# An mLSTM with a feed-forward network on one core: first chunks' decays by TensorE, zeros' products between the groups, a new order of steps

## The chip, the cores and the metric

The kernel runs on one core of one Trainium2 chip. The metric is the device time of one execution in microseconds (us). Five queues work side by side and wait for each other through semaphores: TensorE (PE; its weight loads are PEld), VectorE (DVE), ScalarE (ACT), GpSimd (POOL), and SyncE (SP), which here issues all loads and stores.

## The reference

An mLSTM (4 batches, 8 heads, 768 steps, heads of 40) and behind it a feed-forward network of 320 to 2048 to 320 over all 3072 tokens. Inputs are scaled so that gates reach far into the negative: the exponents must keep full precision.

```python
for t in range(S):
    m_new = np.maximum(f_gate[:, :, t] + m, i_gate[:, :, t])
    f_stab = np.exp(f_gate[:, :, t] + m - m_new)
    i_stab = np.exp(i_gate[:, :, t] - m_new)
    m = m_new
    C = f_stab[..., None, None] * C + i_stab[..., None, None] * np.einsum('bhd,bhe->bhde', vt, kt)
    n = f_stab[..., None] * n + i_stab[..., None] * kt
    h_tilde = np.einsum('bhde,bhe->bhd', C, qt)
    denom = np.maximum(np.abs(np.einsum('bhd,bhd->bh', n, qt)[:, :, None]), 1.0)
    y[:, :, t] = sigmoid(o_gate[:, :, t]) * h_tilde / denom
...
h = x @ w_in                                   # x: y as 3072 tokens of 320
g = np.where(h >= 1, h, np.where(h <= -1, 0.0, (h + 1) ** 2 / 4))
return g @ w_out
```

## The kernel before, in words

**Chunks.** The recurrence is done in chunks of L = 128 steps: 6 chunks of time (c) for each of 4 batches (b), numbered n = 4c + b, 24 in all. Inside a chunk it is a masked attention. `gate_sums(c)` (step g) makes, for all 32 sequences of heads at once, the running maximum m, the clamped log-decays a, and their running sum `ac` (with a rest `al`); `gate_tail` (k) forms four exponents per step in `ex`; `gate_exps` (h) transposes them on TensorE and takes their exponential into G, and the negated sum into nA. The decay between steps s and t is exp(ac[t] − ac[s]) for t ≥ s. For this `ac` is stored to DRAM (`a_d`), and `load_A(n)` (A) loads it back, broadcast over the 128 partitions, as [128, 8 heads, 128]; `select` (e, POOL) puts −30000 where t < s; `decay` (x00, x01: two halves of four heads) adds nA as a bias and takes the exponential on ACT. `score_mm` (s) makes the products of k and q, `score_mul` (m) multiplies them by the decays on DVE, `scale1` (v) scales the values on POOL.

**The rest of a chunk** is the generator `main`: step u multiplies scores by values into `up` (16 narrow fp32 products), y divides by the normalizer and multiplies by the output gate (`sz`, then `y`), z transposes y on TensorE in three pieces, t copies it into `xh` (float32r) and `xl` (what float32r lost). The third piece is 128 columns of which 64 are a copy of columns made by a `tensor_copy` of y.

**The feed-forward part.** Four chunks make a group j of 512 tokens, six groups in all. For each j there are 16 slots fc: `mm1` multiplies by a 128-column piece of w_in into a PSUM bank `psh` (8 products of 512 columns), ACT and DVE apply the activation (r), `parts` splits it into `gh` and `gl`, `mm2` adds to four banks `pso`. The weights come as 64-bit words and are converted on the chip in 16 pieces (`convert`: `words` on ACT, DVE and POOL, then `split` with a cast on ACT and a subtraction on DVE), two of them ahead of the first slot and the others in j = 0. Chunks of the next group are worked on between the slots of the present one by `slot(i)`.

**Order.** The framework's scheduler orders each engine's instructions by a planner's times, except where `InOrder.on` makes every new instruction of an engine follow the one before it. That is so for the front: the list `STEPS` (line 53) is walked by a loop (line 645) that issues loads (L.), the steps above for n = 0 to 3, the gates of the first three chunks of time, two conversions (c), and `warm(k)` (w): k products of zeros (128 x 128 by 128 x 512, bfloat16), of no use for the result. After the list come `load_og(1)`, `load_A(4)` to `load_A(6)` and the first `slot` calls, which follow the last marked copies of step t. All these have line L78 or L81 of the helper in the profile.

**PSUM.** `psum_a` (line 300) hands out banks in the front by turns: two `psa`, one `psh` and four `pso` in a cycle of seven; the eighth bank holds the transposed gates.

Of the kernel before, what the change touches and what calls it, by code (L numbers as in the profile page):

```python
# [51 lines left out]

STEPS = (
# [41 lines left out]
def mlstm_ffn_kernel(ctx, tc, qk, qn, vk, og, fi, w_in, w_out, cst, out):  # L95
# [20 lines left out]


    cs_t = const.tile([P, P + 9 * D1 + 2], F32, name="cs")
    ident = cs_t[:, :P]
    bmask = cs_t[0:120, P:P + 9 * D1].rearrange("p (g x) -> p g x", g=3)  # L120
# [4 lines left out]
    a_d = dr.tile([NSEQ, S], F32, name="a_d")  # L125
# [19 lines left out]
    rst = const.tile([NSEQ, L], F32, name="rst")  # L145

    def load_gates(pool, c0, c1):
        n = (c1 - c0) * L
        sl = slice(c0 * L, c1 * L)
        t = pool.tile([NSEQ, 2, n], F32, name="fi_t", bufs=1 if c0 == 0 else 1)  # L150
        nc.sync.dma_start(t, fi[:, :, sl])
        fg_t, ig_t = t[:, 0, :], t[:, 1, :]
        if c0 == 0:
            nc.gpsimd.memset(rst, 1.0)
            nc.gpsimd.memset(rst[:, 0:1], 0.0)
        for c in range(c0, c1):
            gsrc[c] = pool, ig_t[:, (c - c0) * L:][:, :L], fg_t[:, (c - c0) * L:][:, :L]
# [10 lines left out]
    def gate_sums(c):  # L168
        pool, i, f = gsrc.pop(c)
        new = lambda name, p=NSEQ, n=L, bufs=1: pool.tile([p, n], F32, name=name, bufs=bufs)  # L170
        k = 1
        m, a, ah, ac, al = new("m", n=L + 1, bufs=k), new("a", bufs=k), new("ah", bufs=k), new("ac", bufs=3), new("al", bufs=k)

        ex = exs[c] = new("ex", P, bufs=2)
        nc.vector.tensor_copy(m[:, 0:1], carry)
        nc.vector.tensor_tensor_scan(out=m[:, 1:], data0=f, data1=i, initial=carry, op0=ALU.add, op1=ALU.max)
# [5 lines left out]
        nc.vector.tensor_tensor_scan(out=ac, data0=rst, data1=ah, initial=0.0, op0=ALU.mult, op1=ALU.add)  # L182
# [18 lines left out]
    def gate_exps(c):  # L201
        ex = exs.pop(c)
        if c < 3:
            if c == 0:
                T["gates"] = ps_h.tile([P, 512], F32, name="psh")
            tp = T["gates"][:, c * P:(c + 1) * P]
        else:
            tp = psum_a()[:, :P]
# [61 lines left out]
    def convert(kind, i):  # L270
        raw = raws.pop((kind, i))
        if kind == "in":
# [27 lines left out]
    def psum_a():  # L300
# [80 lines left out]
    def load_A(n):  # L381
# [4 lines left out]
        t["A"] = gate.tile([P, H, L], F32, name="A3") if n == 3 else ld.tile([P, H, L], F32, name="Abc", bufs=3)  # L386
        src = a_d[b * H:(b + 1) * H, c * L:(c + 1) * L]
# [23 lines left out]
    def decay(n, hh):  # L411
# [72 lines left out]
    def main(n):  # L484
# [16 lines left out]
        up = psum_a()  # L501
        if n < SPLIT_FROM:
# [29 lines left out]
        nc.vector.tensor_tensor(out=y[:, :DM].rearrange("p (h d) -> p h d", d=D), in0=hv[:, :, 0:D], in1=sz, op=ALU.mult)  # L532
        nc.vector.tensor_copy(y[:, DM:], y[:, 2 * P:DM])
# [18 lines left out]
        nc.vector.tensor_tensor(out=xh[64:128, 2, cs], in0=xv[64:128, 2, :], in1=xh[64:128, 2, cs].bitcast(F32),  # L552
# [239 lines left out]
```

## Time and profile before

| | |
|---|---|
| median of 3 runs (lowest to highest) | 535.79 us (535.57 to 537.06) |
| the profiled execution | 533.05 us, span of its instructions 531.3 us |
| mean granted clock of TensorE | 0.959 |
| busy: PE, PEld | 496.6 us (93%), 425.4 us (80%) |
| busy: DVE, ACT, POOL | 377.1 us (71%), 300.3 us (57%), 150.8 us (28%) |
| moved by DMA | 53.37 MB |

"Busy" is the time in which an engine has at least one instruction running; instructions of one engine overlap a little, so a sum of durations is some per cent above it. In a row of the timeline the first number is the start in us, the second the time covered, and x7 means seven instructions run together. In a row by stretches come, after the stretch and its length, the busy time and the count of instructions of PE, PEld, DVE, ACT and POOL, then the granted clock, the DMA engines' share and GB/s.

### The profile page before, as it was taken

What the parts mean: (1) busy time and instruction counts of PE and PEld (TensorE: products, weight loads), DVE (VectorE), ACT (ScalarE), POOL (GpSimd) and SP (SyncE); (2) the same over time, 40 slices, a digit from 0 to 9 for tenths busy, and PEclk for the clock granted to TensorE, in tenths of its full rate; (3) what the DMA queues carried; (4) which work ended last, traced back from release to release, by engine and by line L of the source; (5) the groups of instructions that cost most, each with busy time, mean ns of one, the idle gap of its engine ahead of it and who ended that gap; (6) DMA issues with size and microseconds to landing.
All of it is one profiled execution on the core that took longest, in us unless ns stands there. A gap on an engine that the chain in (4) does not pass through costs nothing.

```text
span 531.3 us, 9265 instructions
## 1 busy us (share of the span) xinstructions
PE 496.6 (93%) x3552; PEld 425.4 (80%) x3552; DVE 377.1 (71%) x710; ACT 300.3 (57%) x592; POOL 150.8 (28%) x139
## 2 busy tenths in 40 slices
PE   7976999888998999999999789799999999999996
PEld 3664778867887889879889668688997898989985
DVE  6479799999978677868577749586766676543332
ACT  5635885666586364568363444754459344455553
POOL 1435264251541225342135415034311212000000
PEclk9965899998999999999999989899999999999999
DMA  5997675472431213441213423032433100010001
GB/s 179 319 290 199 177 245 169 134 232 72 149 102 42 55 52 103 133 151 30 68 37 104 118 85 104 11 97 79 114 105 115 40 1 1 1 51 1 0 1 50
DMA packets 51449, 53.37 MB, mean 100 GB/s; under 512 B 10157, under 2 KB 44365, under 8 KB 51405
## 3 DMA queue, kind: packets, MB, share of 16 engines
q1 hardware_dynamic: 51405, 52.78, 32.8%
q8 instruction: 28, 0.46, 0.3%
q14 instruction: 16, 0.13, 0.1%
HBM read 48.72 MB, written 4.06 MB: 99 GB/s over the span
## 4 chain that ended last, share of the span: by engine, by line
PE 64%; DVE 19%; ACT 7%; DMA 4%; issue 3%; POOL 1%; SPq 0%; ACTq 0%; POOLq 0%; DVEq 0%
PE psh L78 28%; PE pso L78 25%; PE psa L78 11%; DVE gl L78 2%; ACT Abc L78 2%; DVE r L78 2%; DVE ow L78 2%; DMA A<-a_d 2%; DVE C L78 1%; ACT r L78 1%; DMA Abc<-a_d 1%; DVE mg L78 1%; DVE win L78 1%; DVE z L78 1%; DVE m L78 1%
## 5 line engine op out<-in xcount | busy, mean ns | idle before, releaser
L78 ACT ACTIVATE r<-psh,half 128x512 f32<-128x512 f32 x96 | 65.4, 685 | 95.0 <-PE psh L78 91.9
L78 PE MATMUL psh<-xh,wh 128*128 128x512 f32 x288 | 105.0, 418 | 9.6 <-DVE r L78 5.2
L78 PE MATMUL pso<-oh,gh 128*128 128x320 f32 x368 | 113.4, 316 | 0.4 <-ACT r L78 0.4
L78 PE MATMUL pso<-ow,gh 128*128 128x320 f32 x368 | 113.3, 312 | 0.0
L78 DVE SCALAR_TENSOR_TENSOR r<-psh,r 128x512 f32<-128x512 f32 x96 | 65.9, 686 | 59.6 <-ACT r L78 59.1
L78 PE MATMUL pso<-oh,gl 128*128 128x320 f32 x368 | 104.7, 311 | 0.0
L78 PE MATMUL psh<-xh,wl 128*128 128x512 f32 x288 | 102.4, 407 | 0.0
L78 DVE TENSOR_TENSOR gl<-r,gh 128x512 fp32r<-128x512 f32 x92 | 71.6, 780 | 31.8 <-ACT gh L78 30.9
L78 ACT CAST gh<-r 128x512 fp32r<-128x512 f32 x92 | 56.8, 618 | 63.5 <-DVE r L78 62.8
L78 PEld LDWEIGHTS pso<-oh,gh 128*128 128x128 f32 x368 | 68.7, 188 | 5.0 <-ACT r L78 0.6
L78 PEld LDWEIGHTS pso<-ow,gh 128*128 128x128 f32 x368 | 69.2, 188 | 3.5
L78 PEld LDWEIGHTS pso<-oh,gl 128*128 128x128 f32 x368 | 66.8, 188 | 0.5
L78 PEld LDWEIGHTS psh<-xh,wh 128*128 128x128 f32 x288 | 51.5, 194 | 18.8 <-DVE r L78 6.5
L78 PEld LDWEIGHTS psh<-xh,wl 128*128 128x128 f32 x288 | 55.7, 195 | 12.3 <-DVE wl L78 0.2
L78 ACT ACTIVATE Abc<-Abc,nA 128x128 f32<-128x128 f32 x160 | 49.3, 389 | 24.8 <-POOL Abc L78 19.4
L78 PE MATMUL psh<-xl,wh 128*128 128x512 f32 x192 | 62.0, 405 | 0.0
L78 ACT ACTIVATE r<-r 128x512 f32<-128x512 f32 x96 | 60.2, 632 | 2.3
L78 POOL TENSOR_TENSOR m<-m 128x1024 bf16<-128x1024 f32 x16 | 32.6, 2037 | 55.4 <-DVE m L78 49.3
L78 POOL TENSOR_TENSOR C<-C,dec 120x369 f32<-120x369 f32 x16 | 14.6, 916 | 106.5 <-PE psa L78 106.5
L78 POOL TENSOR_TENSOR v<-vk,G 128x328 f32<-128x328 f32 x36 | 31.3, 876 | 46.8 <-issue 30.8
L78 PEld LDWEIGHTS psh<-xl,wh 128*128 128x128 f32 x192 | 37.1, 194 | 8.6
L78 PE MATMUL psa<-raw 40*128 40x128 f32 x304 | 30.5, 294 | 0.9 <-DVE hv L78 0.9
(166 smaller groups left out, 723.2 us busy)
## 6 DMA issues: line engine op xcount, KB each, us to landing
Abc<-a_d SPq DMA_DIRECT2D x23, 512.0 KB
raw<-in_qk SPq DMA_DIRECT2D x48, 160.0 KB
vk<-in_vk SPq DMA_DIRECT2D x20, 324.0 KB
wraw<-in_w_in SPq DMA_DIRECT2D x8, 768.0 KB
wraw<-in_w_out SPq DMA_DIRECT2D x8, 640.0 KB
sig<-in_og SPq DMA_DIRECT2D x6, 640.0 KB
out<-r SPq DMA_DIRECT2D x24, 160.0 KB
qn<-in_qn SPq DMA_DIRECT2D x20, 180.0 KB
```

The lines of the kernel that those rows point to most:

```text
L78: r = getattr(self.engine, name)(*args, **kwargs)
```

## The change

1. **Decays of chunks 0 to 3.** The first gates are loaded on 96 partitions (`fi0`: the 32 sequences three times). The sums `ac` stand there three times; two subtractions of the upper 16 bits (`top`) leave in the three blocks the three bfloat16 parts of the sum. `exponents(b)` (A0 to A3) puts into PSUM the mask (identity times `late_t`, −30000 where t < s) and adds, per head, a product of `pick`, which chooses the head's three rows, with the three parts. `decay` then reads PSUM. `first_sums` (p) transposes the sums for nA, which DVE reads. No store, broadcast load or `select` is left for these chunks; the others keep them, from an `a_d` whose rows of one chunk of time lie together.
2. **Zeros' products.** Instead of `warm` at a place of its own, `heat` is set by w and `hot(out)` issues that many zeros' products at the beginning of the next group, into the bank that the group then overwrites. The list has w9, w3 and then ones and twos between nearly all groups.
3. **Order.** The list is new. The second and third chunks' gates (k1, h1, g2, k2, h2) and the second conversion stand behind t3; the conversion is parted into c (words) and d (split), both in order.
4. **y.** It has 320 columns; the third transposition takes its last 128, so the copy goes, and the last subtraction of t writes the other half of `xh`'s third block. For c = 0 POOL makes `sz`.
5. **Smaller.** First chunk's copies into `ex` on POOL instead of ACT, one more copy into `ex` there for all chunks; `ident` and the block mask are loaded separately; psum_a's cycle is eight banks, with two of `psh`.

```diff
 STEPS = (
-    "w8 w2 Lf Lc Lo Lq0 g0 k0 A0 Lq1 o A2 h0 A1 w8 Lv0 Lq2 Lw0 s0 w6 Lq3 w2 w3 Lv2 A3 s1 g1 e0 "
-    "v0 x00 k1 Lw1 x01 m01 m00 w2 e1 v1 x10 x11 m10 u0 s2 e2 v2 x21 e3 c m11 y0 x20 m20 w4 m21 v3 u1 "
-    "w7 s3 y1 x31 z0 x30 t0 u2 z1 m31 w2 m30 u3 w1 y2 t1 c y3 z2 t2 h1 z3 g2 k2 w1 t3 w4 h2 "
+    "Lg Lo Li Lq0 Lv0 Lq1 Lw0 Lf Lq2 Lv2 Lq3 Lw1 Lc o w9 g0 p w3 A0 k0 x00 w1 s0 m00 w1 A1 h0 x01 v0 m01 x10 w1 s1 "
+    "v1 m10 x11 m11 w2 u0 w2 A2 y0 c x20 w1 s2 x21 v2 m20 w1 u1 z0 m21 w2 t0 y1 g1 d w2 A3 x30 w1 s3 x31 v3 m30 w1 u2 "
+    "z1 m31 w2 t1 y2 w1 u3 z2 w2 t2 y3 z3 w2 t3 k1 h1 c d g2 k2 h2 "
 )
...
-    a_d = dr.tile([NSEQ, S], F32, name="a_d")
+    a_d = dr.tile([NC, NSEQ, L], F32, name="a_d")
...
+    def first_gates():
+        t = gate.tile([3 * NSEQ, 2, L], F32, name="fi0")
+        nc.sync.dma_start(t, fi0)
+        gsrc[0] = gate, t[:, 1, :], t[:, 0, :]
...
-        nc.sync.dma_start(a_d[:, c * L:(c + 1) * L], ac)
-        nc.scalar.copy(ex[64:96], ac)
+        if c > 0:
+            nc.sync.dma_start(a_d[c], ac)
+            nc.scalar.copy(ex[64:96], ac)
+        else:
+            for p in (2 * NSEQ, NSEQ):
+                nc.vector.tensor_tensor(out=ac[:p], in0=ac[:p], in1=top(ac[:p]), op=ALU.subtract)
+            T["ac"] = ac
+            m, a, ah, ac, al, i = (x[2 * NSEQ:] for x in (m, a, ah, ac, al, i))
+            nc.gpsimd.tensor_copy(ex[64:96], ac)
...
+    def top(x):
+        return x.bitcast(BF16).rearrange("p (t w) -> p t w", w=2)[:, :, 1]
+
+    def first_sums():
+        tp = psum_a()
+        hot(tp)
+        tp = tp[:, :NSEQ]
+        nc.tensor.transpose(tp, T["ac"][2 * NSEQ:], ident[2 * NSEQ:3 * NSEQ, 2 * NSEQ:3 * NSEQ])
+        nc.vector.tensor_scalar(out=nA[:, 0, :], in0=tp, scalar1=-1.0, scalar2=None, op0=ALU.mult)
+
+    def exponents(b):
...
+        ps = T[n]["Ap"] = [psum_a() for _ in range(2)]
+        hot(ps[0])
+        for hh in range(2):
+            nc.tensor.matmul(ps[hh], idb, late_t.unsqueeze(1).broadcast_to([P, 4, P]), start=True, stop=False)
+        for hh in range(2):
+            for h in range(4):
+                k = b * H + 4 * hh + h
+                nc.tensor.matmul(ps[hh][:, h * L:(h + 1) * L], pick[:, k:k + 1].broadcast_to([3 * NSEQ, P]),
+                                 top(T["ac"]), start=False, stop=h == 3)
...
-    def warm(k):
-        out = psum_a()
-        for _ in range(k):
+    heat = 0
+    def hot(out):
+        nonlocal heat
+        for _ in range(heat):
             nc.tensor.matmul(out, zeros[:, :P], zeros, start=True, stop=True)
+        heat = 0
...
-            nc.scalar.activation(A[:, h, :], A[:, h, :], AF.Exp, bias=bias)
+            src = T[n]["Ap"][hh][:, (h - 4 * hh) * L:][:, :L] if c == 0 else A[:, h, :]
+            nc.scalar.activation(A[:, h, :], src, AF.Exp, bias=bias)
...
-        nc.vector.tensor_tensor(out=sz, in0=sg.rearrange("p (h d) -> p h d", d=D),
+        mark["x", "pool"] = (nc.vector if c else nc.gpsimd).tensor_tensor(out=sz, in0=sg.rearrange("p (h d) -> p h d", d=D),
                                                      in1=z.unsqueeze(2).broadcast_to([P, H, D]), op=ALU.mult)
-        y = wk.tile([P, 3 * P], F32, name="y", bufs=2)
...
-        nc.vector.tensor_copy(y[:, DM:], y[:, 2 * P:DM])
...
-        for k in range(3):
+        hot(xp)
+        for k in range(2):
             nc.tensor.transpose(xp[:, k * P:(k + 1) * P], y[:, k * P:(k + 1) * P], ident)
+        nc.tensor.transpose(xp[:, 2 * P:3 * P], y[:, DM - P:], ident)
...
         elif what[0] == "c":
-            mark["c", "act"], mark["c", "dve"] = nc.scalar.last, nc.vector.last
-            InOrder.on = False
-            split_next("c")
-            InOrder.on = True
+            rest = convert(*W_ORDER[nw])
+            load_w(*W_ORDER[nw + 2])
+            nw += 1
+        elif what[0] == "d":
+            rest()
```

More of the change, by code (lines that the diff above doesn't have):

```diff
@@ L94, in mlstm_ffn_kernel @@
 @with_exitstack
-def mlstm_ffn_kernel(ctx, tc, qk, qn, vk, og, fi, w_in, w_out, cst, out):
+def mlstm_ffn_kernel(ctx, tc, qk, qn, vk, og, fi0, fi, w_in, w_out, cst, out):
     nc = Core(tc)
@@ L115, in mlstm_ffn_kernel @@
     nc.gpsimd.memset(zeros, 0.0)
-    cs_t = const.tile([P, P + 9 * D1 + 2], F32, name="cs")
-    ident = cs_t[:, :P]
-    bmask = cs_t[0:120, P:P + 9 * D1].rearrange("p (g x) -> p g x", g=3)
+    ident = const.tile([P, P], F32, name="ident")
+    cs_t = const.tile([120, 9 * D1], F32, name="cs")
+    bmask = cs_t.rearrange("p (g x) -> p g x", g=3)
+    idb = gate.tile([P, P], BF16, name="idb")
+    nc.gpsimd.affine_select(out=idb, in_=zeros[:, :P], pattern=[[1, P]], compare_op=ALU.not_equal, fill=1.0,
+                            base=0, channel_multiplier=-1)
+    pick = gate.tile([3 * NSEQ, NSEQ], BF16, name="pick")
+    for g in range(3):
+        nc.gpsimd.affine_select(out=pick, in_=pick if g else zeros[:3 * NSEQ, :NSEQ], pattern=[[1, NSEQ]],
+                                compare_op=ALU.not_equal, fill=1.0, base=g * NSEQ, channel_multiplier=-1)
+    late_t = gate.tile([P, P], BF16, name="late_t")
+    nc.gpsimd.affine_select(out=late_t, in_=zeros[:, :P], pattern=[[1, P]], compare_op=ALU.is_ge, fill=-30000.0,
+                            base=0, channel_multiplier=-1)
     half = const.tile([P, 1], F32, name="half")
     nc.vector.memset(half, 0.5)
-    a_d = dr.tile([NSEQ, S], F32, name="a_d")
+    a_d = dr.tile([NC, NSEQ, L], F32, name="a_d")
     G = const.tile([P, NC, P], F32, name="G")
@@ L202, in gate_exps @@
         ex = exs.pop(c)
[L203 to L208, printed above, removed]
+        tp = psum_a()[:, :P]
         nc.tensor.transpose(tp, ex, ident)
         nc.scalar.activation(G[:, c, :], tp, AF.Exp)
-        nc.scalar.mul(nA[:, c, :], tp[:, 64:96], -1.0)
         if c > 0:
+            nc.scalar.mul(nA[:, c, :], tp[:, 64:96], -1.0)
             decays(c, c + 1)
+    def top(x):
[7 more added lines that the diff above has]
+    def exponents(b):
+        n = b
+        T.setdefault(n, {})["A"] = (gate.tile([P, H, L], F32, name="A3") if n == 3 else
+                                    ld.tile([P, H, L], F32, name="Abc", bufs=3))
+        ps = T[n]["Ap"] = [psum_a() for _ in range(2)]
[7 more added lines that the diff above has]
+                                 top(T["ac"]), start=False, stop=h == 3)
     def decays(c0, c1):
@@ L275, in convert @@
             words(w, raw)
-            split(wh[:, :, sl], wl[:, :, sl], w)
+            return lambda: split(wh[:, :, sl], wl[:, :, sl], w)
         else:
@@ L280, in convert @@
             if 2 * i >= PLAIN_FC:
-                split_out(i)
+                return lambda: split_out(i)
+        return lambda: None
     def split_out(i):
@@ L385, in load_A @@
         t = T.setdefault(n, {})
-        t["A"] = gate.tile([P, H, L], F32, name="A3") if n == 3 else ld.tile([P, H, L], F32, name="Abc", bufs=3)
-        src = a_d[b * H:(b + 1) * H, c * L:(c + 1) * L]
+        t["A"] = ld.tile([P, H, L], F32, name="Abc", bufs=3)
+        src = a_d[c, b * H:(b + 1) * H]
         mark[n, "A"] = nc.sync.dma_start(t["A"], src.unsqueeze(0).broadcast_to([P, H, L]))
@@ L501, in main @@
         up = psum_a()
+        hot(up)
         if n < SPLIT_FROM:
@@ L647, in mlstm_ffn_kernel @@
         hh = int(what[2:] or 0)
-        if what == "Lf":
-            load_gates(gate, 0, 3)
+        if what == "Lg":
+            first_gates()
+        elif what == "Lf":
+            load_gates(gate, 1, 3)
         elif what == "Lc":
-            nc.sync.dma_start(cs_t, cst)
+            nc.sync.dma_start(cs_t, cst[0:120, P:])
+        elif what == "Li":
+            nc.sync.dma_start(ident, cst[:, :P])
         elif what == "Lo":
@@ L670, in mlstm_ffn_kernel @@
         elif what[0] == "A":
-            load_A(n)
+            exponents(n)
+        elif what[0] == "p":
+            first_sums()
         elif what[0] == "v":
@@ L675, in mlstm_ffn_kernel @@
             sigmoid(0)
-        elif what[0] == "e":
-            select(n)
         elif what[0] == "x":
@@ L699, in mlstm_ffn_kernel @@
     for i in range(FRONT - EARLY, FRONT):
-        with behind(("x", "act"), ("x", "dve")):
+        with behind(("x", "act"), ("x", "dve"), ("x", "pool")):
             slot(i)
```

66 lines of the change are left out of this document (39 added, 27 removed).

## The prediction

> **What bounds the kernel now.** I read the page's slices first, then busy times by stretch, then the chain that ended last in the opening stretch.
>
> ```profile
> span 531.3 us, 9265 instructions
> ...
> PEclk9965899998999999999999989899999999999999
> ```
> ```profile
> core 0: us, PE busy (x) PEld busy (x) DVE busy (x) ACT busy (x) POOL busy (x), PEclk, DMA share, GB/s
> 0.00:51.74 51.74, 41.32 (x218) 26.27 (x219) 35.65 (x98) 25.94 (x68) 20.93 (x26) 0.80 0.85 253
> 51.74:139.60 87.86, 82.06 (x477) 69.56 (x476) 83.27 (x136) 61.31 (x120) 33.82 (x31) 0.95 0.52 165
> 139.60:216.00 76.40, 74.33 (x573) 65.81 (x572) 58.03 (x109) 46.22 (x90) 24.94 (x21) 1.00 0.27 80
> ```
>
> The first row is the front, the part that the step list orders: it ends when the last copy of the fourth chunk (step t3) is made, at 51.74. The second row is the first 16 feed-forward slots (they end where ACT finishes its 16th reading of a product, 139.60); in it DVE is busy 83.27 of 87.86 us, idle only 4.59. That stage converts the weights on DVE, so it ends when DVE's list is done. In the third row DVE is at 58.03 of 76.40 and TensorE at 74.33: from there TensorE leads. So what the change is worth is read from one balance: DVE's work up to 139.60 is 35.65 + 83.27 = 118.92, its idle time 16.09 + 4.59 = 20.68. A front that ends earlier helps only as far as one of the two shrinks.
>
> ```profile
> 5.49 2.76 DMA a_d<-ac
> ...
> 10.07 7.49 DMA Abc<-a_d
> 17.57 10.11 DMA A<-a_d
> ...
> 28.87 2.44 ACT A L81 x8
> ```
>
> These are rows of the chain of waits: the sums go to DRAM (5.49) and return broadcast; the fourth chunk's copy lands only at 27.68, and eight exponentials take 2.44. The change removes these trips.
>
> **The change part by part: DVE's work.** Durations are of this execution (span 531.3, its own time 533.05, the median of the runs shown 535.79, so 2.74 above it).
>
> ```profile
> L81 DVE TENSOR_TENSOR sz<-sig,z 128x320 f32<-128x320 f32 x4 | 2.2, 560 | 0.1
> ...
> L81 DVE COPY y<-y 128x64 f32<-128x64 f32 x4 | 0.8, 194 | 0.1
> ```
> ```profile
> 10.49 0.28 DVE L81 TENSOR_TENSOR a<-fi_t,m 32x128 f32<-32x128 f32 x1
> ...
> 11.93 0.15 DVE L81 TENSOR_TENSOR dc<-ac,al 32x1 f32<-32x1 f32 x1
> ...
> 37.53 0.86 DVE L78 TENSOR_SCALAR win<-wraw 128x768 uint16<-128x768 uint16 x1
> 38.29 1.08 DVE L78 TENSOR_SCALAR mg<-mg 128x768 f32<-128x768 f32 x1
> ...
> 39.48 0.95 DVE L78 SCALAR_TENSOR_TENSOR win<-mg,win 128x768 int32<-128x768 int32 x1
> ...
> 41.62 1.27 DVE L78 TENSOR_TENSOR wl<-win,wh 128x768 fp32r<-128x768 f32 x1
> ...
> 43.45 3.34 POOL L78 TENSOR_SCALAR_AFFINE_SELECT Abc<-Abc 128x1024 f32<-128x1024 f32 x3
> ...
> 44.19 0.14 DVE L81 COPY m<-carry 32x1 f32<-32x1 f32 x1
> ...
> 45.86 1.06 DVE L81 TENSOR_TENSOR a<-a,m 32x128 f32<-32x128 f32 x1
> ...
> 50.82 0.15 DVE L81 TENSOR_TENSOR dc<-ac,al 32x1 f32<-32x1 f32 x1
> ...
> 51.44 0.29 DVE L81 TENSOR_TENSOR xh<-pso,xh 64x128 fp32r<-64x128 f32 x1
> ```
>
> Gone from DVE: four copies of y in the front (0.8) and four more before 139.60 (another 0.8), and four products sz that POOL takes (2.2). New: two subtractions that part the sums (0.28 each, like row 10.49, since only the partitions grow) and nA read on DVE (0.15 by row 11.93), less one small copy (0.14): +0.6. Net −3.2. Merely moved behind t3: the tail of the second chunk's gates (10.49 to 12.08, 1.6), the second weight conversion (0.86 + 1.08 + 0.95 + 1.27 = 4.2) and the third chunk's gates (44.19 to 50.97, 6.8). They free t3 but stay on DVE's list, so I credit them at nothing; what would be lost if they weren't covered is those 12.6 us, now due between t3 and the sixteenth slot. POOL's masking of the later chunks goes with them: row 45.86 shows a DVE step of 0.28 taking 1.06 while the three masks of row 43.45 run. Four masks vanish from POOL, but they ran mostly while DVE waited. I carry that slowing over unchanged, bounded by 3.3 us either way (the three masks' length).
>
> **DVE's idle time in the new front.** Every engine keeps the step list's order, so I walk the queues with these rows.
>
> ```profile
> 1.72 3.19 PE L81 MATMUL psa<-zeros 128*128 128x512 bf16 x7
> ...
> 11.44 2.08 PE L81 MATMUL pso<-raw 40*128 40x128 f32 x16
> ...
> 20.31 0.74 POOL L81 TENSOR_TENSOR ow<-ow,G 128x328 f32<-128x328 f32 x1
> ...
> 24.93 1.68 PE L81 MATMUL pso<-zeros 128*128 128x512 bf16 x7
> ...
> 26.54 1.16 PE L81 MATMUL pso<-raw 40*128 40x128 f32 x16
> ...
> 28.02 1.88 PE L81 MATMUL psa<-ow,Abc 128*128 128x41 f32 x16
> ...
> 35.30 3.63 PE L81 MATMUL pso<-ow,A 128*128 128x41 f32 x16
> ...
> 40.03 0.48 ACT L81 CAST xh<-pso 128x384 fp32r<-128x384 f32 x1 [5.05 <-PE pso L81]
> ```
> ```profile
> DVE m L81 <- DMA fi_t<-in_fi: 2.3, 1, 2.3
> ```
>
> The pairs show each product at half and at full clock: a zeros' product 0.43 or 0.24, a score group 2.08 or 1.16, a chunk's output group 3.63 or 1.88. No row has the new exponents' products. They are bfloat16 as the zeros are, two of 512 columns and eight of 128, so I estimate by columns (0.43 and a quarter of it): 1.7 at half clock, 1.0 at full. Both ends: 0.9 (weights hidden) and, if each of the ten cost as much as a zeros' product, 4.3; the zeros are the nearest row. The waits that follow:
>
> 1. Start: the sums wait for their gates as now, 0.8 + 2.3 = 3.1.
> 2. Chunk 0. The sums' parts are ready at about 6.1. TensorE then has a transposition (as one zeros' product, 0.43), three zeros (1.3) and the exponents (1.7): the first half at 9.1. ACT's four exponentials, half of 2.44, end at 10.3. DVE's gate work ends at 8.6; with the score group behind, it waits 2.6. ACT's next entry is the gates' exponential, and TensorE reaches its transposition only after scores 0 and the next exponents, at 12.5 to 14.5; so x01 waits too, and DVE 2.3 again, then twice 0.5 (1.22 on ACT against 0.69 on DVE). Together 5.9.
> 3. sz on POOL: y's last step waits for it, and DVE with all that is queued behind y (conversion, gates, score products). 0.74 to 0.9 and two handovers: 1.0 four times, 4.0.
> 4. On ACT the second chunk's two copies of sums (g1) and the weight cast (d) stand ahead of x30, so chunk 3's exponentials start near 30 although its exponents are in PSUM at 24: DVE waits 1.1 for the cast and 0.8 for the two halves.
> 5. Transposition, cast (0.48) and handovers ahead of t2 and t3: 1.2 each, 2.4.
> 6. While ACT is late, TensorE has nothing from about 28 to 33, and I expect half clock from there: +1.2.
>
> Sum 3.1 + 5.9 + 4.0 + 1.9 + 2.4 + 1.2 = 18.5, against 16.1 now. DVE's work up to t3 is 35.65 − 1.6 − 4.2 − 6.8 − 2.4 = 21, so t3 ends near 40 instead of 51.74. Loads don't set it: 253 GB/s moved in the first row, and the first four chunks' loads, with 2 MB of broadcasts gone, are 4.6 MB, in by some 20 us. SP's queue loses four issues that waited for the sums' store; fi0, ident and cs are three small ones more. The relaid a_d merges rows of 512 B; its later loads hide behind 0.52 of DMA share.
>
> After t3:
>
> ```profile
> DVE Abc L78 <- PE psa L78: 1.5, 1, 1.5
> ...
> 53.55 1.22 PE L78 MATMUL psh<-xh,wh 128*128 128x512 f32 x2 [0.21 <-DVE Abc L78]
> ```
>
> Now DVE idles 4.59 there, 1.5 of it for the next chunk's scores at a cold clock. With 12.6 us of backlog at hand I take 3.0 (ends 1.0 and 4.6).
>
> **The sum.** 118.9 − 3.2 + 18.5 + 3.0 = 137.2 for 139.6: 2.4 earlier. Behind it sixteen copies of y go, 16 × 0.194 = 3.1 of DVE time where TensorE leads; a quarter counts, 0.8. Together 3.2 us: 529.9 for the profiled 533.05, and 532.6 beside the median. About 0.3%, 1.6 us, is what a measurement of this kernel can tell from no change.
>
> **The clock.**
>
> ```profile
> 3.38:6.79 3.41, 2.39 (x6) 0.60 (x4) 3.09 (x12) 0.94 (x3) 0.00 (x0) 1.00 0.93 336
> ...
> 13.60:17.03 3.43, 3.43 (x9) 1.22 (x8) 1.24 (x2) 2.10 (x8) 0.00 (x0) 1.00 1.24 303
> ...
> 27.27:30.68 3.41, 2.93 (x29) 2.57 (x27) 2.30 (x7) 1.81 (x7) 2.03 (x2) 1.00 0.81 255
> 30.68:57.99 27.31, 20.37 (x77) 14.74 (x79) 23.26 (x52) 14.38 (x44) 10.75 (x10) 0.50 0.71 210
> ```
>
> The record shows a clock of 1.00 from the start, but the zeros' 0.43 says half; it rises after the stretch 13.60 to 17.03, which zeros and scores filled, and falls after 27.27 to 30.68, though TensorE was busy 2.93 of 3.41 with narrow products. Two to three zeros a group may not be enough to raise it or hold it. The Trainium skill, TensorE: Matmul & The Clock Gate, Part 1, says that one busy window of about 3.4 us lifts the gate and one idle window lowers it again. By that rule the clock would hold until the pause at 28, as step 6 has it; the trace disagrees on the fall, which came after a window 86% busy, and that speaks for the second rival below.
>
> **The rivals.**
> - *TensorE, not DVE, sets the first stage.* It is busy 82.06 of 87.86 there, which speaks for it; that its loads are busy 69.56 (79%) against 65.81 of 76.40 (86%) in the next stage speaks against. Then the first product's start counts: 53.55 becomes some 42 to 44, and allowing for a cold start the gain is 8 to 9: about 527. It needs DVE's backlog to fit in the gaps.
> - *The clock stays at half through the front (slower).* Place: between chunk 0's exponents and u3. The doubled groups are then 4 × (0.7 + 0.9 + 1.75) + 28 zeros × 0.19 + transpositions 4 × 0.3 = 20 us more on TensorE, which becomes the front's bound: t3 near 52, DVE idle near 29 instead of 18.5, so 10.4 later than the sum, 543; if it falls only from 20 us on, about 537 to 539. It decides once DVE's idle exceeds 23.5. For: the fall at 30.68. Against: more zeros in the gaps than in that window, which had none.
> - *Nothing to measure.* The removed trip is replaced by waits 2 to 4 in full and the clock rises as late as 17: idle 20 to 22, 534.5 to 537.
> - *The exponents' products don't shorten chunk 0* (each ten cost 4.3): 2.6 more in step 2 and again in part for chunk 1; this is inside the case before.
>
> **How the numbers follow.** Forecast 0.43 (own range 529.5 to 534); TensorE's case 0.15; nothing to measure 0.22; half clock 0.20. Faster 0.58, same 0.22, slower 0.20. The range 527 to 539 takes in the first three and the milder part of the last, and leaves out some 0.06 below and 0.12 above.
>
> **What would show it.** Right: no load of the sums for chunks 0 to 3, t3 near 40, the first wide product near 42, DVE idle 17 to 20 up to t3 with waits on POOL of 0.8 to 1.0 four times, the sixteenth slot read near 137. Wrong: zeros' products of 0.43 behind 20 us (the clock), t3 far from 40, or DVE idle by more than 5 us between t3 and the sixteenth slot, which would mean that TensorE sets the stage.

## The result, and the profile after

The changed kernel takes 552.45 us (median of 4 runs, 548.6 to 554.7) against 536.42 for the kernel before (4 runs, 535.57 to 537.53): a ratio of 1.029, with an interval of 1.0216 to 1.0364. It is slower by 16 us, where 3 us less were forecast, and lies 13 us above the range. The profiled execution took 550.32 us, its span is 548.5.

The page of the changed kernel, its span and the granted clock in 40 slices:

```profile
span 548.5 us, 9300 instructions
...
PEclk9956579998899999999999979999999999999999
```

The same kernel by stretches: the front up to the last copy t3, the first 16 feed-forward slots, and the rest. In between stands one stretch of the second row by itself.

```profile
core 0: us, PE busy (x) PEld busy (x) DVE busy (x) ACT busy (x) POOL busy (x), PEclk, DMA share, GB/s
0.00:42.95 42.95, 30.71 (x210) 21.27 (x210) 23.58 (x67) 16.62 (x44) 14.85 (x30) 0.82 0.75 224
42.95:155.50 112.55, 91.46 (x504) 76.11 (x505) 93.04 (x159) 68.52 (x139) 40.50 (x39) 0.84 0.44 141
52.53:66.04 13.51, 0.00 (x1) 0.03 (x1) 11.64 (x26) 6.79 (x16) 6.50 (x5) 0.58 0.60 202
155.50:548.52 393.02, 373.59 (x2861) 329.75 (x2859) 254.60 (x461) 212.86 (x406) 95.08 (x86) 0.98 0.22 66
```

t3 ends at 42.95 instead of 51.74, 8.8 us earlier. The 16th slot is read at 155.50 instead of 139.60, 15.9 later, and the rest takes 393.02 instead of 391.68. So the front gained, and the stage behind it lost 24.7. DVE's work up to the 16th slot is 23.58 + 93.04 = 116.62 (118.92 before). Its idle time is 42.95 − 23.58 = 19.37 up to t3 and 112.55 − 93.04 = 19.51 behind it, where before had 4.59. The third row shows the largest pause of TensorE: 13.51 us in which it does nothing.

Rows from the timeline of that place, sorted by start (start, us covered, engine, line, operation; in brackets the idle time before it and what ended it):

```profile
42.66 0.29 DVE L82 TENSOR_TENSOR xh<-psh,xh 64x128 fp32r<-64x128 f32 x1
...
46.23 1.20 PE L79 MATMUL psh<-xh,wh 128*128 128x512 f32 x2
...
47.79 5.65 ACT L79 ACTIVATE Abc<-Abc,nA 128x128 f32<-128x128 f32 x19
48.93 0.96 DVE L82 SCALAR_TENSOR_TENSOR win<-mg,win 128x768 int32<-128x768 int32 x1
52.13 0.40 PE L79 MATMUL psh<-xh,wl 128*128 128x512 f32 x1
53.35 0.81 ACT L82 CAST wh<-win 128x768 fp32r<-128x768 f32 x1
54.19 0.96 DVE L82 TENSOR_TENSOR wl<-win,wh 128x768 fp32r<-128x768 f32 x1 [4.31 <-ACT wh L82]
55.07 0.13 DVE L82 COPY m<-carry 32x1 f32<-32x1 f32 x1
...
65.61 0.28 DVE L82 TENSOR_TENSOR ex<-m,ah 32x128 f32<-32x128 f32 x1
66.04 0.45 PE L82 MATMUL pso<-ident,ex 128*128 128x128 f32 x1 [13.51 <-DVE ex L82]
66.52 0.28 ACT L82 ACTIVATE G<-pso 128x128 f32<-128x128 f32 x1 [2.20 <-PE pso L82]
67.27 2.08 PE L79 MATMUL pso<-raw 40*128 40x128 f32 x16
68.39 1.24 ACT L79 ACTIVATE r<-psh,half 128x512 f32<-128x512 f32 x2
```

Read it as a chain over three queues. The second conversion's words are ready at 49.9 (`win` on DVE), but ACT's cast `wh` stands behind 19 exponentials of later chunks and starts at 53.35. DVE waits 4.31 for it, and its list holds the third gates (from `m<-carry`, 55.07) behind the subtraction `wl`. Mixed with conversions of other weights the gates' chain runs until 65.9 (`ex`). Then TensorE gets the transposition of these gates (step h2), for which it has stood still since 52.5. Behind h2 in its queue are the next chunk's scores (67.27), and on ACT behind G the activation of slot 0 (68.39), although the products of the first two slots were done by 52.5. The Trainium skill, TensorE: Matmul & The Clock Gate, Part 2 (step-by-step), says that matmuls stay in program order and only weight loads are pulled ahead; this trace agrees, with 13.51 us of idle TensorE ahead of one 0.45 us transposition.

The pause itself is not where DVE loses most of its time:

```profile
42.95:52.53 9.58, 8.71 (x25) 6.58 (x25) 5.48 (x11) 5.92 (x21) 3.49 (x6) 0.56 0.30 72
66.04:76.00 9.96, 9.26 (x37) 6.83 (x38) 8.73 (x13) 8.26 (x13) 4.06 (x4) 0.54 0.58 166
76.00:100.00 24.00, 24.00 (x136) 19.71 (x135) 13.58 (x25) 12.70 (x25) 4.44 (x6) 1.00 0.24 83
```

Of the 19.51 us, 4.10 lie ahead of 52.53, 13.51 − 11.64 = 1.87 in the pause, 1.23 from there to 76, and 24.00 − 13.58 = 10.42 between 76 and 100; 1.9 come later. Between 76 and 100 TensorE is busy without a gap, ACT waits 9.7 for its products and DVE 5.6 for ACT's part of the activation. The weights are not converted meanwhile: the subtraction that ends a conversion stands on DVE at 78.19 and then not before 104.64, while the kernels h2_late, c2_free and g2_first below make four or five of them in that time. So what the chain held up is paid for after it, when TensorE catches up and DVE's list has little that can go. That last step is read from this trace and no run isolates it.

### The profile page after: what moved, and what is told of

It reads as the page before. It is cut to its first block, busy times and chain, and to the rows that moved or that the text cites. A ratio compares the mean times of both kernels' runs of the same rounds, so it can differ in the third digit from the quotient of the medians.

```text
span 548.5 us, 9300 instructions
## 1 busy us (share of the span) xinstructions
PE 495.8 (90%) x3573; PEld 427.1 (78%) x3573; DVE 371.2 (68%) x685; ACT 298.0 (54%) x588; POOL 150.4 (27%) x152
## 4 chain that ended last, share of the span: by engine, by line
PE 60%; DVE 15%; DMA 10%; ACT 9%; issue 2%; POOL 2%; SPq 1%; ACTq 0%; DVEq 0%; POOLq 0%
PE psh L79 26%; PE pso L79 23%; PE psa L79 10%; ACT Abc L79 4%; DMA Abc<-a_d 3%; DMA wraw<-in_w_in 2%; ACT r L79 2%; DVE r L79 2%; DMA vk<-in_vk 2%; DMA out<-r 2%; DMA wraw<-in_w_out 1%; DVE gl L79 1%; DVE z L79 1%; DVE mg L79 1%; DVE ow L79 1%
## 5 line engine op out<-in xcount | busy, mean ns | idle before, releaser
L79 PE MATMUL psh<-xh,wh 128*128 128x512 f32 x288 | 105.3, 422 | 14.6 <-DVE r L79 5.5
L79 DVE SCALAR_TENSOR_TENSOR r<-psh,r 128x512 f32<-128x512 f32 x96 | 65.9, 687 | 69.0 <-ACT r L79 68.6
L79 DVE TENSOR_TENSOR gl<-r,gh 128x512 fp32r<-128x512 f32 x92 | 69.6, 759 | 31.8 <-ACT gh L79 31.0
L79 PEld LDWEIGHTS psh<-xh,wh 128*128 128x128 f32 x288 | 52.3, 196 | 24.2 <-DVE r L79 6.8
L79 ACT ACTIVATE Abc<-Abc,nA 128x128 f32<-128x128 f32 x160 | 49.1, 389 | 18.5 <-POOL Abc L79 18.5
```

The costliest lines, as they stand in the source:

```text
L79: r = getattr(self.engine, name)(*args, **kwargs)
```

## The balance of all kernels

The ledger of the prediction (DVE's work, its idle time up to t3 and from there to the reading of the 16th slot), worked out for each profiled execution as above. Ratios are to the kernel before, run beside each of them on the same chip; for the rows below the first two its medians were 533.82 to 534.86 us.

| kernel | median us | ratio [95%] | t3 | idle to t3 | idle after | work | 16th slot | rest |
|---|---|---|---|---|---|---|---|---|
| before | 536.42 | 1 | 51.7 | 16.1 | 4.6 | 118.9 | 139.6 | 391.7 |
| after | 552.45 | 1.029 [1.0216, 1.0364] | 43.0 | 19.4 | 19.5 | 116.6 | 155.5 | 393.0 |
| h2_late | 538.27 | 1.0068 [1.0035, 1.0102] | 44.6 | 21.0 | 7.3 | 120.6 | 148.9 | 387.9 |
| g2_free | 538.49 | 1.0076 [1.0039, 1.0113] | 45.3 | 21.7 | 6.1 | 120.4 | 148.2 | 388.4 |
| c2_free | 535.51 | 1.0026 [1.0, 1.0053] | 44.0 | 20.4 | 9.0 | 116.6 | 146.0 | 386.9 |
| g2_first | 533.22 | 0.9975 [0.9942, 1.0008] | 49.5 | 17.0 | 6.9 | 117.0 | 140.9 | 389.2 |
| b_tail | 537.65 | 1.0082 [1.0049, 1.0116] | 51.2 | 21.3 | 3.4 | 120.6 | 145.3 | 389.8 |
| sz_dve | 530.41 | 0.9915 [0.9882, 0.9948] | 48.2 | 13.8 | 8.3 | 116.4 | 138.5 | 391.3 |
| c2_sz | 531.19 | 0.9914 [0.9882, 0.9946] | 37.8 | 12.8 | 7.0 | 116.8 | 136.5 | 390.5 |
| nozero | 540.84 | 1.0101 [1.006, 1.0142] | 58.0 | 25.4 | 4.3 | 117.3 | 146.9 | 392.8 |
| hotter | 539.12 | 1.0089 [1.0057, 1.0121] | 51.3 | 18.6 | 7.8 | 117.9 | 144.2 | 395.0 |
| hot_u3 | 532.5 | 0.9966 [0.9939, 0.9993] | 46.6 | 11.8 | 9.6 | 118.7 | 140.1 | 389.1 |
| x3_first | 534.74 | 1.0006 [0.9982, 1.003] | 46.1 | 11.1 | 7.8 | 118.8 | 137.7 | 393.5 |
| b_nocopy | 539.52 | 1.0085 [1.0052, 1.0118] | 52.3 | 16.8 | 4.4 | 120.0 | 141.1 | 393.8 |
| c2_sz_dummy | 532.91 | 0.9963 [0.9928, 0.9997] | 40.4 | 13.6 | 7.7 | 117.4 | 138.7 | 393.6 |

One reserve: the last column should be alike where the work is alike, and it runs from 387 to 395. The planner orders that part anew for every kernel, and this spread limits what an edit of the front can be read for. Where a verdict below hangs on the front, the columns before it are read too.

## The experiments: the stage behind t3

**h2_late.** The third gates' transposition and exponentials alone leave the list.

```diff
-"... t3 k1 h1 c d g2 k2 h2 "
+"... t3 k1 h1 c d g2 k2 "
     # after the loop over the first slots
+    with behind(("x", "act"), ("x", "dve"), ("x", "pool")):
+        gate_exps(2)
```

> The changed kernel (list tail c d g2 k2 kept in the list, in this order) with only h2, the third gates' transposition on TensorE and the exponentials behind it, taken out of the list and made in free order behind the first slots. DVE's list keeps c d g2 k2. Q as a matter of TensorE's and ACT's queues alone: the pause of 13.5 us goes and the time falls to 536 to 541, as where all of the third gates were freed (538.5). If instead DVE's order is what costs (g2 behind the subtraction that waits for ACT's cast), the time stays within 4 us of 552.

Idle time after t3 falls from 19.5 to 7.3, and 1.029 becomes 1.0068. The 16th slot is read at 148.9 instead of 155.5, 6.6 earlier; the rest is 5.1 shorter, which the front doesn't explain. So h2's place in the list was a plug. What it held up shows in the trace of this kernel:

```profile
51.13 1.16 PE L79 MATMUL psa<-raw 40*128 40x128 f32 x14
55.39 0.81 ACT L82 CAST wh<-win 128x768 fp32r<-128x768 f32 x1
55.47 1.95 PE L79 MATMUL psa<-v,Abc 128*128 128x41 f32 x16 [0.36 <-DVE Abc L79]
65.72 1.58 PE L79 MATMUL psa<-ow 128*120 128x123 f32 x6 [8.30 <-POOL ow L79]
72.25 0.45 PE L79 MATMUL pso<-ident,ex 128*128 128x128 f32 x1 [0.99 <-DVE ex L82]
73.31 1.23 ACT L79 ACTIVATE r<-psh,half 128x512 f32<-128x512 f32 x2
```
```profile
76.00:100.00 24.00, 23.35 (x109) 18.13 (x109) 20.31 (x29) 15.90 (x24) 7.43 (x7) 0.90 0.48 145
```

The cast is as late as before behind the same 19 exponentials, TensorE stands still for 8.30 again (now for POOL), and h2 and slot 0's activation come even later than in the changed kernel (72.25 and 73.31 against 66.04 and 68.39). So neither the pause nor the late start of slot 0 is by itself what costs. The difference is that the next chunks' scores (51.13) and output products (55.47; the changed kernel has such products only at 86.73) no longer stand behind h2, and that DVE is busy for 20.31 us between 76 and 100 instead of 13.58. The clock doesn't tell the two apart: it was granted at 0.50 between 66 and 76 here, and at 0.54 in the changed kernel.

**g2_free.** All three steps of the third gates (g2, k2, h2) leave the list and are issued behind the first slots with `gate_piece(2)`.

```diff
-"... t3 k1 h1 c d g2 k2 h2 "
+"... t3 k1 h1 c d "
     # after the loop over the first slots
+    with behind(("x", "act"), ("x", "dve"), ("x", "pool")):
+        gate_piece(2)
```

> The changed kernel with one thing moved: the third chunk's gates (g2, k2, h2) are taken out of the step list and made by gate_piece(2), in free order, behind the first slots ahead of the feed-forward part. Nothing else differs. Theory Q (queues): the changed kernel lost its time because TensorE's queue stood 13.5 us (52.5 to 66.0) at the transposition of these gates, and ACT's at their exponential, with the next chunks' scores and the first slots' activations queued behind. Then the pause goes and the sixteenth slot is read 10 to 15 us earlier: 537 to 543. Theory C (clock): the front's clock fell at 27.4 us and stayed at half until 75 but for one window, and that is what costs; the pause only shows it. Then the clock record and the time change little: 549 to 554. Theory D (DVE's list): the same work on DVE in another order, 550 to 554.

1.0076, nearly as h2_late: the gates' work on DVE was no more harmful in order than out of it; h2 was what counted of the three. In both kernels DVE does some 4 us more ahead of the 16th slot than in the changed kernel (120.4 to 116.6), work that the planner drew forward.

**c2_free.** The second conversion alone leaves the order; the gates stay in it.

```diff
-"... t3 k1 h1 c d g2 k2 h2 "
+"... t3 k1 h1 g2 k2 h2 "
     # after the list
+    mark["c", "act"], mark["c", "dve"] = nc.scalar.last, nc.vector.last
     InOrder.on = False
+    split_next("c")
```

> The changed kernel with the second weight conversion (c, d behind t3) taken out of the list and made in free order after it, as the kernel before did; g2 k2 h2 stay in the list. Q: g2 no longer stands behind the subtraction that waited until 54.2 us for ACT's cast, which itself stood behind 19 exponentials of the next chunks; h2 is reached some 8 to 10 us earlier and the pause shrinks to 3 to 5 us: 540 to 546. C: no change, 549 to 554. D: no change.

1.0026: most of the loss is gone with the conversion that started the chain. The timeline of ACT, with no cast behind the exponentials:

```profile
48.03 3.32 ACT L79 ACTIVATE Abc<-Abc,nA 128x128 f32<-128x128 f32 x11
...
55.96 0.25 ACT L82 ACTIVATE G<-pso 128x128 f32<-128x128 f32 x1
...
57.09 1.23 ACT L79 ACTIVATE r<-psh,half 128x512 f32<-128x512 f32 x2
```

G comes at 55.96 instead of 66.52 and slot 0's activation at 57.09 instead of 68.39, 11 us earlier, with h2 in its place in TensorE's queue. So neither h2's place alone nor the conversion's alone (h2_late) makes the whole loss: that takes the two together, gates in order behind a conversion in order that waits for ACT. Neither edit brings the front back, though. The 16th slot is read at 146.0 here and at 148.9 in h2_late, 6.4 and 9.3 later than in the kernel before; that the ratios lie near 1 is also due to a rest that is 4.8 and 3.8 shorter than there.

**g2_first.** The gates go ahead of t3, as the kernel before has g2 and k2.

```diff
-"... t2 y3 z3 w2 t3 k1 h1 c d g2 k2 h2 "
+"... t2 y3 z3 k1 h1 g2 k2 w2 t3 h2 c d "
```

> The changed kernel with the tail of the list as the kernel before had it in spirit: t2 y3 z3 k1 h1 g2 k2 w2 t3 h2 c d, so both gates stand ahead of t3 on DVE and the transposition h2 waits for less. Q: t3 comes some 7 us later (near 50), but TensorE is not held for 13 us afterwards; the two nearly cancel or gain: 540 to 548. C: no change, 549 to 554. D (what counts is the sum of DVE's work): no change, 549 to 554.

0.9975 [0.9942, 1.0008]: all of the loss is gone, with t3 7 us later than in the changed kernel (49.46 against 42.95). Here 14.6 of the 15.9 us come back ahead of the 16th slot.

```profile
0.00:49.46 49.46, 32.67 (x224) 22.66 (x224) 32.44 (x89) 20.29 (x59) 18.77 (x35) 0.77 0.65 201
49.46:140.90 91.44, 85.31 (x498) 72.13 (x497) 84.58 (x137) 64.44 (x126) 34.13 (x33) 0.94 0.54 171
```

Slot 16 is read at 140.90, and of that 117.02 is DVE's work and 23.88 its idle time. t3 at 42.95 was worth nothing, t3 at 49.46 costs nothing. With the plug out, the change is within what can be told from no change.

**b_tail.** The move of the change in the kernel before, where the conversion is not in order: g2 and k2 go behind t3.

```diff
-"... z3 g2 k2 w1 t3 w4 h2 "
+"... z3 w1 t3 w4 g2 k2 h2 "
```

> The kernel before with one thing moved: g2 k2 stand behind t3 (list's end: z3 w1 t3 w4 g2 k2 h2), as in the changed kernel. Everything else is as before. Q: t3 is some 7 us earlier, and if h2's transposition again stands ahead of the next chunk's scores TensorE waits for it; 536 to 544, no gain of 7. If the order alone were good (the idea of the change): 529 to 533. C: 536 to 537.

1.0082, and idle after t3 is 3.4: here the gates behind t3 plug nothing. The loss lies ahead of t3:

```profile
0.00:51.20 51.20, 39.26 (x217) 25.76 (x218) 29.88 (x82) 24.87 (x64) 20.04 (x26) 0.80 0.86 251
51.20:145.30 94.10, 85.46 (x480) 70.93 (x479) 90.74 (x158) 63.58 (x126) 33.67 (x31) 0.94 0.54 167
```

```profile
DVE xl L81 <- ACT xh L81: 6.3, 2, 5.3
```

DVE's work to t3 falls by 5.8, but t3 comes only 0.5 earlier: the row of DVE's waits between 25 and 51.2 (6.3 us in all, twice, 5.3 the longest) shows one of 5.3 ahead of the last copies, which the gates filled before. The idle time to t3 grows from 16.1 to 21.3, and behind t3 the gates cost their time.

## The experiments: the front

**sz_dve.** g2_first with `sz` on DVE for all chunks.

```diff
-        mark["x", "pool"] = (nc.vector if c else nc.gpsimd).tensor_tensor(out=sz, ...
+        mark["x", "pool"] = nc.vector.tensor_tensor(out=sz, ...
```

> The kernel g2_first with sz of the first four chunks on DVE again instead of POOL. By the walk of the queues DVE works 0.56 us four times more and no longer waits about 0.9 to 1.0 (2.5 and more where POOL masks a later chunk just then) four times: 1.5 to 5 us earlier, 528.5 to 532. If DVE's list is what counts and its waits are filled otherwise: 2 later, 535.

0.9915 against 0.9975. In g2_first DVE's wait for POOL is

```profile
DVE y L82 <- POOL sz L82: 5.9, 4, 3.3
```

(5.9 us in all, four times, 3.3 the longest); in the changed kernel it was 5.3, with one of 2.6, because POOL's mask of a later chunk, which had waited for its load, ran ahead of that `sz`:

```profile
38.41 1.09 POOL L79 TENSOR_SCALAR_AFFINE_SELECT Abc<-Abc 128x1024 f32<-128x1024 f32 x1 [4.20 <-DMA Abc<-a_d]
39.47 0.72 POOL L82 TENSOR_TENSOR sz<-sig,z 128x320 f32<-128x320 f32 x1
40.23 0.49 DVE L82 TENSOR_TENSOR y<-psa,sz 128x320 f32<-128x320 f32 x1 [2.64 <-POOL sz L82]
```

With `sz` on DVE the wait is gone and the idle time to t3 falls from 17.0 to 13.8:

```profile
0.00:48.20 48.20, 34.86 (x225) 24.10 (x226) 34.40 (x93) 22.29 (x65) 16.45 (x31) 0.82 0.69 206
48.20:138.50 90.30, 82.67 (x476) 68.22 (x474) 82.00 (x134) 60.41 (x113) 34.85 (x31) 0.94 0.53 172
```

Handing 2.2 us of DVE's work to POOL thus cost more than it saved. The intervals of the two ratios just touch; the next run has the same edit with intervals well apart.

**c2_sz.** c2_free with the same edit.

> The kernel c2_free (the changed kernel's list with only the second conversion made free; 535.5) with sz on DVE. If the wait for POOL is a term of its own, worth what it gave in the other order (2.8): 532 to 533.5. If the two mendings are one and the same: 535 to 536.

0.9914 [0.9882, 0.9946] against 1.0026 [1.0, 1.0053] for c2_free: the same edit, worth 4.3 us here. t3 ends at 37.8, the 16th slot at 136.5, the earliest of all, and yet the time is that of sz_dve, whose t3 ends 10 us later. From t3 to the 16th slot DVE is busy here for 91.73 of 98.70 us and TensorE for 84.50:

```profile
37.80:136.50 98.70, 84.50 (x488) 70.70 (x489) 91.73 (x157) 65.84 (x133) 38.55 (x36) 0.92 0.50 162
```

**nozero.** g2_first with no zeros' product in the list.

> The kernel g2_first (the changed kernel with both gates ahead of t3, 533.2) without any of the zeros' products; only they are left out. Theory C: the clock never rises in the front, TensorE's groups double and the time rises by 6 to 10 us, to 539 to 543. Theory W (waits for other engines set the front; TensorE is idle for a third of it anyway): the zeros' own 6 to 9 us on TensorE fall away, the slower groups take it back, 532 to 537.

1.0101: without them 7.6 us more, t3 at 58.0 instead of 49.5, DVE's idle time to t3 25.4 instead of 17.0 (3.1 of it a longer wait for POOL's `sz`, 9.0 against 5.9). Stretches of 3.41 us of this kernel (of the engines only PE):

```profile
core 0: us, PE busy (x), PEclk, DMA share, GB/s
...
6.82:10.23 3.41, 3.41 (x26) 1.00 1.07 317
...
27.28:30.69 3.41, 3.41 (x24) 1.00 0.75 270
```
```profile
7.83 2.08 PE L80 MATMUL pso<-raw 40*128 40x128 f32 x16
...
27.11 2.08 PE L80 MATMUL pso<-raw 40*128 40x128 f32 x16
```

From 6.82 to 30.69 all seven stretches are full, and still a group of scores takes 2.08 at the end as at the beginning, the price at half clock (1.16 at full). The record's 1.00 only means that no change was noted yet; the first is noted at 61.6, after the wide products (first pair 60.34, 1.20) begin. The zeros are what raises the clock in the front: nothing else was taken out.

**hotter.** g2_first with more zeros where the clock was low.

```diff
-"... w1 u3 ... y3 z3 ..."
+"... w16 u3 ... y3 w12 z3 ..."
```

> The kernel g2_first with more zeros where TensorE pauses: sixteen instead of one ahead of u3, twelve instead of none ahead of z3. C: the clock, which fell at 26.5 us, holds or rises again before the first wide products; u3 takes 1.9 instead of 3.6 us and the first slots run at full clock: 528 to 531. W: the waits stay, 532 to 535; if the zeros outlast the pauses, 1 to 2 more.

1.0089, slower than g2_first by 5.9 us. The zeros ahead of z3 ran at half clock:

```profile
34.64 4.52 PE L80 MATMUL psh<-zeros 128*128 128x512 bf16 x12
41.01 0.55 PE L80 MATMUL psh<-ident,y 128*128 128x128 f32 x3 [1.85 <-DVE y L80]
```

They did not stand in the way of z3, which waited 1.85 more for y behind them and then took 0.55 (0.90 in g2_first). t3 is 1.8 later mostly because y waits longer for POOL's `sz` (2.02 and 3.73 for the last two chunks, 0.91 and 3.29 in g2_first); what the zeros have to do with that is not shown. The 16th slot is 3.3 later. That the rest is 5.8 longer is not explained.

**hot_u3.** sz_dve with twelve zeros ahead of u3 and no others added.

```diff
-"... w1 u3 ..."
+"... w12 u3 ..."
```

> The kernel sz_dve with twelve zeros instead of one ahead of u3, in TensorE's pause of 3.7 us there, and no others added. At full clock they take 2.6 us and fit. If the clock then holds through u3 and z2 (3.6 and 0.9 fall to 1.9 and 0.5): 1 to 2 us faster, 528.5 to 529.5. If it falls all the same the twelve take 5.2 us and u3 is late: 1 to 3 us slower, 531.5 to 533.5.

```profile
24.83 2.75 PE L80 MATMUL psa<-zeros 128*128 128x512 bf16 x11
28.96 2.03 PE L80 MATMUL psa<-ow,A 128*128 128x41 f32 x16 [1.39 <-DVE A L80]
```
```profile
31.21 3.60 PE L82 MATMUL psa<-ow,A 128*128 128x41 f32 x16 [4.82 <-DVE A L82]
```
```profile
30.54 3.15 PE L82 MATMUL psa<-ow,A 128*128 128x41 f32 x16 [3.69 <-DVE A L82]
```

The clock holds: u3 takes 2.03 (3.60 in the changed kernel, 3.15 in sz_dve, the second and third fence), t3 is 1.6 earlier and the idle time to t3 2.0 less than in sz_dve. But idle after t3 is 1.3 more and work 2.3 more, and the ratio is 0.9966 against 0.9915. A faster TensorE at this place gave nothing.

**x3_first.** sz_dve with step g1 and the split d moved behind m31, to let chunk 3's exponentials start earlier on ACT (step 4 of the prediction's walk).

```diff
-"... y1 g1 d w2 A3 ... z1 m31 w2 ..."
+"... y1 w2 A3 ... z1 m31 g1 d w2 ..."
```

> The kernel sz_dve (both gates ahead of t3, sz on DVE; 530.4) with g1 and d moved behind m31, so that ACT's copies of the second chunk's sums and its weight cast no longer stand ahead of chunk 3's exponentials. By the walk of the queues (step 4 of the prediction) DVE loses its waits for the cast and the halves, 1.2 + 0.3 to 1.9 us, and TensorE's pause of 3.7 us ahead of u3 shrinks: 527.5 to 529.5. If the front's waits only move to another place: 529.5 to 531.5.

Idle to t3 falls to 11.1, as step 4 has it, and the 16th slot is read 0.8 earlier, but the time is 1.0006 against 0.9915, slower by 4.3 in the medians. The loss doesn't lie in the front: the rest is 393.5 against 391.3 in the profiled executions, which differ by only 1.4 in all. Its cause stays open.

## The experiments: the copy of y

**b_nocopy.** The kernel before with only the fourth part of the change.

```diff
-        y = wk.tile([P, 3 * P], F32, name="y", bufs=2)
...
-        nc.vector.tensor_copy(y[:, DM:], y[:, 2 * P:DM])
+        y = wk.tile([P, DM], F32, name="y", bufs=2)
...
-        for k in range(3):
+        for k in range(2):
             nc.tensor.transpose(xp[:, k * P:(k + 1) * P], y[:, k * P:(k + 1) * P], ident)
+        nc.tensor.transpose(xp[:, 2 * P:3 * P], y[:, DM - P:], ident)
...
-        nc.vector.tensor_tensor(out=xh[64:128, 2, cs], in0=xv[64:128, 2, :], in1=xh[64:128, 2, cs].bitcast(F32),
+        nc.vector.tensor_tensor(out=xh[0:64, 2, cs], in0=xv[64:128, 2, :], in1=xh[64:128, 2, cs].bitcast(F32),
                                 op=ALU.subtract)
```

> The kernel before with only the copy of y taken out (320 columns, third transposition of the last 128, the subtraction into the other half of xh's third block). DVE's list up to the sixteenth slot is 1.6 us shorter: 1 to 2.4 us faster than before. If the copies lie in DVE's waits: no difference within 1 us.

1.0085 [1.0052, 1.0118]: slower, with 24 copies less. DVE's work ahead of the 16th slot is 120.0, where 118.9 less seven copies (0.8 + 0.6) would be 117.5, so other work was drawn forward; that slot is 1.5 later and the rest 2.1 longer.

**b_dummy, c2_sz_dummy.** b_nocopy and c2_sz with a copy of the same size into a tile that nothing reads.

```diff
+        yy = wk.tile([P, D1 + 23], F32, name="yy", bufs=1)
+        nc.vector.tensor_copy(yy, y[:, 2 * P:])
```

> The kernel b_nocopy (the kernel before without the copies of y, 539.5) with a copy of the same size again in the same place, but into a tile that nobody reads: 24 times 0.2 us of DVE without any use. If the copies' absence costs because the planner then orders DVE, ACT and TensorE differently, and the copy only brings the old order back: 534 to 537, faster for more work. If the new third transposition or the subtraction into the other half of the block costs by itself: 539.5 to 542. If both orders differ and the order is luck: anywhere between.

> The kernel c2_sz (531.2) with the same useless copy. By DVE's list alone: eight copies up to the sixteenth slot and sixteen later, 0.8 to 2.4 later, 532 to 533.6. If the absence of the copy costs in this kernel too by another order: 526 to 530.

b_dummy is 1.0038 [1.0, 1.0076]: with useless work put back, the kernel is faster rather than slower than b_nocopy. That speaks against the new transposition as the cost and for the order that the planner makes, but the intervals overlap a little, so it is not settled. c2_sz_dummy is 0.9963 [0.9928, 0.9997] against 0.9914 [0.9882, 0.9946]: there the copies cost 1.7 us in the medians, within the 0.8 to 2.4 that the list of DVE's work gives; these intervals overlap too. The profiled execution of b_dummy lies near the top of its runs (541.0 for a median of 535.42) and isn't read.

## Why the prediction was wrong, by its own steps

**The balance held.** That the end of the 16th slot is DVE's work plus its idle time is a mere identity, but the reading from it, that a t3 that ends earlier is worth nothing by itself, was shown: t3 at 37.8 (c2_sz) and at 48.2 (sz_dve) give the same ratio.

**DVE's work** was forecast at 115.7 and measured 116.6. One small term was misread: between 51.74 and 139.6 the kernel before makes three copies of y (72.13, 96.46, 120.58) and not four. The copies' share shows in c2_sz_dummy, with overlapping intervals, and not in b_nocopy.

**The walk of the front** came out: idle to t3 18.5 forecast, 19.37 measured; t3 near 40 forecast, 42.95 measured. The work up to t3 was 23.6 instead of 21, though in total only 0.9 more. The terms are near as well and not only their sum: 2.8 against 3.1 for the start (2.0 for the gates and 0.8), 5.4 against 5.9 for chunk 0 and the one behind it, 1.5 against 1.9 in step 4, 3.0 against 2.4 in step 5. The exponents were priced at 1.7 at half clock and 1.0 at full, and took 1.91 and 1.06:

```profile
7.32 1.06 PE L82 MATMUL psh<-late_t,idb 128*128 128x512 bf16 x2
8.17 1.06 PE L82 MATMUL psh<-ac,pick 96*128 96x128 bf16 x8
...
11.26 0.59 PE L82 MATMUL pso<-late_t,idb 128*128 128x512 bf16 x2
11.70 0.62 PE L82 MATMUL pso<-ac,pick 96*128 96x128 bf16 x8
```

Step 3, `sz` on POOL, was right in kind and too small: 5.3 against 4.0 in the changed kernel, 7.9 in c2_free. The prediction saw two handovers and not the mask that POOL may run first. Taken out it gives 2.8 to 4.3 us. Step 6 has the place: the clock is at half from 27.4, where TensorE stops. It did not see how long: half clock lasts until 75.2, but for one window of 3.41 us.

**The step that failed** is "with 12.6 us of backlog at hand I take 3.0 (ends 1.0 and 4.6)", with "I credit them at nothing" ahead of it. The measured idle time after t3 is 19.51, 16.5 more, and the measured time is off by 20.4 us in the profiled execution (550.32 against 529.9); the rest, 393.0 instead of 390.9, is 2.1 more of it and work and front 1.8. The error was to treat the moved steps, credited at nothing, as DVE's work alone. k1, h1, c, d, g2, k2 and h2 also put instructions into the queues of ACT, POOL and TensorE, in an order that nothing may pass, between the first products and everything that follows. The bounds 1.0 and 4.6 were those of before, where no conversion stands in order ahead of h2. The question "what is queued behind h2 on TensorE, and what must have happened before h2 can go" wasn't asked; the answer is the chain above, and behind it the 10.42 us between 76 and 100. b_tail shows that gates moved in the old front give 3.4 of idle time after t3, the forecast size. In the new front the term was too small even without the chain: the ten runs that have zeros and break the chain lie between 6.1 and 9.6. By that difference, as an estimate, 3 to 7 of the 16.5 belong to the new front as such and 10 to 13 to the chain.

**The sign named for failure** (DVE idle by more than 5 us after t3) came, but its reading, "TensorE sets the stage", is right for a part only: TensorE is busy 91.46 of 112.55 there and idle for 21. It sets the stretch from 76 to 100, with 24.00 of 24.00, after it had itself waited 13.51 for DVE; in the whole stage the engines waited in turn.

**The rivals.** "The clock stays at half" had the right price for the wrong kernel: without any zeros the loss is 7.6 us with t3 at 58.0 and 25.4 us of idle time (10.4, 52 and 29 forecast). With the zeros of the change the clock is full from 10.4 to 27.4 and then at half to t3, so the milder form of this rival did come. It is not the cause of the loss: g2_first has the clock at half from 26.5 to 53.8 and loses nothing, and in hot_u3 a full clock for u3 gained nothing. "TensorE sets the stage" would have needed a time of 527 from an early first product, and c2_sz has that product at 40.7 and takes 531.19, with TensorE idle for 14.2 of the 98.7 us behind t3. "Nothing to measure" is what the change is once the chain is broken (g2_first), with waits 2 to 4 in the place of the removed trips, as that rival has it; its idle time of 20 to 22 was priced up to t3, and g2_first has 17.0.

## What to carry to other kernels

A step moved in an in-order list must be priced on every queue that it issues to: for each engine write down what stands behind its instruction there, and what has to finish, on which other queues, before it can go. A handover of a small piece of work to a quieter engine costs two handovers plus whatever that engine's queue may run first, which here was more than the work saved. When a gain in one stage is expected, check first that the stage's end is set by what is shortened: ten microseconds of earlier t3 were worth nothing, and removed waits of six to eight on DVE's list were worth three to four. And a pause that shows in a trace is not yet the loss: h2_late keeps one of 8.30 and a later first slot, and is 0.7% behind instead of 2.9%; look at where the engine that bounds the stage has nothing to do.

## What the hardware showed that was not expected

A TensorE that is fully busy need not get its full clock. In nozero seven stretches of 3.41 us in a row are 3.41 busy (first and last above), with narrow fp32 products and, for about 2 us of each chunk, the exponents' bfloat16 products. The score groups stay at 2.08, and the rise is noted at 61.6, behind wide products that begin at 60.34. In the changed kernel, with nine zeros, then three, then one to two a group, the clock is full from 10.4 on, and the scores at 17.60 take 1.16; it is at half again from 27.4. The Trainium skill, TensorE: Matmul & The Clock Gate, Part 1, says that about 3.4 us of a busy TensorE lift the gate; by these rows it depends on what TensorE is busy with. And a change far ahead of it, or one copy more or less per chunk, goes with shifts of several microseconds either way in the 390 us behind the 16th slot, with nearly the same work in it; which of the planner's choices does it was not found.
